# A new instruction order, a wider choice of engines, and a last output tile in two column halves, in clustered attention followed by a softplus feed-forward layer

## The chip, the cores and the metric

The kernel runs on one core of one Trainium2 chip. The metric is the device time of one execution in microseconds (us). The kernel before takes 824.29 us, the median of three runs (823.51 to 825.02). Engines are called PE (TensorE matmul), PEld (TensorE weight load), DVE (VectorE), ACT (ScalarE), POOL (GpSimd) and SP (SyncE, which here issues every DMA).

## The reference, cut to what matters

Attention with 4 batches, 8 heads, 768 positions and head size 64; a query sees only the keys that fall to the same one of 16 centroids. Its output, as 3072 tokens of 512, goes through a feed-forward layer of width 2048 with a softplus.

```python
mask = q_assign[:, :, :, None] == k_assign[:, :, None, :]
scores = scale * np.matmul(q, k.transpose(0, 1, 3, 2))
scores = np.where(mask, scores, -1000000000.0)
attn = np.exp(scores - np.max(scores, axis=-1, keepdims=True))
attn = attn / (np.sum(attn, axis=-1, keepdims=True) + 1e-09)
attn_out = np.matmul(attn, v)
x = attn_out.transpose(0, 2, 1, 3).reshape(B * S, H * D)
h = x @ w_in
g = np.maximum(h, 0.0) + np.log1p(np.exp(-np.abs(h)))
return g @ w_out
```

## The kernel before

Numbers of 32 bits are split into a high and a low half of 16 bits, so that a product takes three matmuls. Attention is done in 192 tiles of 128 queries by 768 keys (a "tile t" below), in 8 passes of 24 tiles; one pass is one batch and half of its positions. The heads of batch 0 are prepared at the start with transposes on PE (`turn` with `on_chip`), all later ones with DMA transposes (`flip`). The first 24 tiles are done in 32 bits with transposes on PE (`whole`, L992); the later ones transpose their probabilities by DMA (`pt<-phl`). The feed-forward layer of a pass runs beside the attention of the next one: `ffn1` (L1222) gives a piece h of 128 features, `softplus` (L1247) makes g of it on ACT, DVE and POOL, `ffn2` (L1304) multiplies by w_out, one half of the features at a time, and `store` (L1328) scales the result out of PSUM and sends it. The very last work is the tile i = 2 of the last pass, second half: 24 matmuls of 512 columns, one DVE instruction (L1339) and one DMA of 256 KB (L1342).

The order of all instructions is written out: every step of the work is a generator ("chain"), each `yield op(...)` is one step, and the list `SEQUENCE` names, one after another, the chain whose next step is emitted. A code is 1000 times the number of the engine chosen plus the number of the chain. So 465 is the next step of the first matrix (two steps for each of 128 pieces), 466 the next of the second, and 1465 cannot occur since such a step has one engine only. Chain 0 prepares the centroids, 1 to 48 are the loads and preparations of k, q and v, 49 to 432 are `scores(t)` and `attend(t)` in turn, 433 to 464 the weights (`prep_weights`, L626), and from 467 on stand chains that others spawn. Every engine takes its instructions in this order and waits by semaphores where its input is not there. The class `Order` (L269) follows the list with planned durations; its outcome matters for the code only through `warm` (L487), which puts small matmuls ("fill", L494) where PE is planned to idle.

Steps with a choice in the kernel before: `evict` (PSUM to SBUF copy, ACT or DVE, L514), `sub` (low half, POOL or DVE, L524), `cast` (high half, ACT, DVE or POOL, L534), the shift in `prep_weights` (L669, DVE or ACT), and three steps of `softplus` (L1263 to L1285). Steps with one engine only: the scaling in `prep_weights` (L663, ACT), the copy of k's high half (L822, ACT), the scaling of q (L918, ACT) and the product of q with its cluster flag (L977, POOL). In `prep_q` the step before L977 gives the flag `aq` (L968, DVE), and the step beside it writes the mask (L971, DVE); `prep_k` writes k's mask at L839 (DVE).

Of the kernel before, what the change touches and what calls it, by code (L numbers as in the profile page):

```python
# [19 lines left out]
SW2 = 256.0  # L20
# [8 lines left out]
WIDE = 1  # L29
EBIAS = 200  # L30
# [1384 lines left out]
```

## Time and profile before

| what | value |
|---|---|
| device time, median of 3 (lowest to highest) | 824.29 us (823.51 to 825.02) |
| profiled execution: span from first to last instruction | 824.5 us; what lies around it is not on the page |
| busy: PE, PEld, DVE, ACT, POOL | 98%, 63%, 79%, 69%, 54% |
| granted TensorE clock, mean | 0.998 |
| chain that ended last | PE 79%, DMA 4%, DVE 3%, ACT 3%, POOL 1%, issue 1% |

The page describes one profiled execution. "Busy" is the share of the span in which an engine has at least one instruction running; PE's matmuls overlap, so their durations add up to more than the busy time. A row of the waits says which engine sat idle, at which line, and which instruction ended the idle time.

### The profile page before, as it was taken

How to read it: one execution, taken by the hardware profiler on the slowest of the kernel's cores; microseconds unless marked ns; L12 is line 12 of the kernel's file. 1: busy time of each engine (PE TensorE's matmuls, PEld its weight loads, DVE VectorE, ACT ScalarE, POOL GpSimd, SP SyncE). 2: the span in 40 equal slices, each digit the busy share in tenths (PEclk: the TensorE clock that was granted, in tenths of full speed). 3: DMA queues.
4: the chain of work that ended last, by engine and by line, in shares of the span. 5: the costliest groups of instructions: out<-in, count | busy, mean ns of one | idle time of the engine just before them, and what ended most of it. 6: DMA issues, size and time to landing. Idle time of an engine off the chain costs nothing.

```text
span 824.5 us, 19467 instructions
## 1 busy us (share of the span) xinstructions
PE 809.5 (98%) x7893; PEld 518.3 (63%) x7893; DVE 647.6 (79%) x1127; ACT 567.8 (69%) x987; POOL 444.5 (54%) x358
## 2 busy tenths in 40 slices
PE   8999988999999999999999999999999999999998
PEld 7888865655656565656565656656666565555553
DVE  8999999998898977898778888887587887743222
ACT  7999998998857667667565746785686664433530
POOL 4325444655367376777685465856777653522320
PEclk9999999999999999999999999999999999999999
DMA  9436999999979999999978989999969874640001
GB/s 327 161 85 168 214 201 228 205 225 177 207 153 187 180 195 205 195 211 193 180 141 155 173 174 183 211 212 175 201 135 169 163 135 103 123 84 14 26 2 38
DMA packets 386314, 134.27 MB, mean 163 GB/s; under 512 B 362672, under 2 KB 379056, under 8 KB 386224
## 3 DMA queue, kind: packets, MB, share of 16 engines
q1 hardware_dynamic: 386224, 133.03, 80.1%
q8 instruction: 61, 1.00, 0.5%
q14 instruction: 29, 0.24, 0.1%
HBM read 35.68 MB, written 6.29 MB: 51 GB/s over the span
## 4 chain that ended last, share of the span: by engine, by line
PE 79%; DMA 4%; DVE 3%; ACT 3%; POOL 1%; issue 1%; DVEq 0%; ACTq 0%; POOLq 0%
PE s L1021 11%; PE h L1236 9%; PE h L1237 9%; PE h L1238 9%; PE o L1321 9%; PE o L1319 9%; PE o L1320 9%; DMA pt<-phl 4%; PE mbank L1157 3%; PE mbank L1159 3%; PE mbank L1158 3%; DVE negm L1037 1%; ACT p L1048 1%; DVE phl L529 1%; ACT phl L539 1%
## 5 line engine op out<-in xcount | busy, mean ns | idle before, releaser
L1048 ACT ACTIVATE p<-s,negm 128x768 f32<-128x768 f32 x190 | 171.9, 908 | 77.9 <-DVE negm L1037 65.6
L1037 DVE TENSOR_REDUCE negm<-s 128x1 f32<-128x768 f32 x192 | 181.7, 951 | 35.4 <-PE s L1021 34.2
L529 POOL TENSOR_TENSOR phl<-p,phl 128x768 f16<-128x768 f32 x81 | 138.2, 1710 | 71.7 <-DVE phl L539 36.0
L1238 PE MATMUL h<-xT,wi 128*128 128x384 f16 x512 | 166.8, 326 | 0.0
L1237 PE MATMUL h<-xT,wi 128*128 128x384 f16 x512 | 166.8, 326 | 0.0
L1236 PE MATMUL h<-xT,wi 128*128 128x384 f16 x512 | 166.7, 326 | 0.0
L1021 PE MATMUL s<-kt,qt 128*128 128x384 f16 x768 | 156.1, 326 | 2.5 <-DVE phl L1111 1.4
L1321 PE MATMUL o<-wo,gh 128*128 128x512 f16 x384 | 146.0, 380 | 0.0
L1320 PE MATMUL o<-wo,gh 128*128 128x512 f16 x384 | 146.0, 380 | 0.0
L1319 PE MATMUL o<-wo,gh 128*128 128x512 f16 x384 | 146.0, 380 | 0.0
L1285 POOL TENSOR_TENSOR fg<-fg,fa 128x384 f32<-128x384 f32 x64 | 69.8, 1094 | 82.9 <-ACT fa L1281 74.9
L1157 PE MATMUL mbank<-vb,pt 128*128 128x65 f16 x1008 | 109.0, 193 | 3.0 <-DMA pt<-phl 3.0
L1158 PE MATMUL mbank<-vb,pt 128*128 128x64 f16 x1008 | 109.1, 192 | 0.0
L1159 PE MATMUL mbank<-vb,pt 128*128 128x65 f16 x1008 | 108.8, 194 | 0.0
L1157 PEld LDWEIGHTS <-pt 128*128 128x128 f16 x1008 | 93.7, 98 | 16.8 <-DMA pt<-phl 5.1
L1021 PEld LDWEIGHTS <-qt 128*128 128x128 f16 x768 | 71.9, 98 | 48.9 <-issue 3.5
L1158 PEld LDWEIGHTS <-pt 128*128 128x128 f16 x1008 | 93.1, 97 | 11.4
L1267 ACT ACTIVATE fa<-h 128x384 f32<-128x384 f32 x82 | 40.2, 491 | 80.7 <-PE h L1238 63.8
L529 DVE TENSOR_TENSOR phl<-p,phl 128x768 f16<-128x768 f32 x81 | 90.6, 1125 | 4.3 <-ACT phl L539 2.2
L1159 PEld LDWEIGHTS <-pt 128*128 128x128 f16 x1008 | 93.2, 97 | 0.0
L539 ACT CAST phl<-p 128x768 f16<-128x768 f32 x92 | 75.2, 828 | 8.3 <-DMA pt<-phl 7.7
L1280 ACT ACTIVATE fa<-fa 128x384 f32<-128x384 f32 x128 | 65.8, 522 | 11.2 <-DVE fa L1263 11.1
(176 smaller groups left out, 1474.0 us busy)
## 6 DMA issues: line engine op xcount, KB each, us to landing
wo<-in_moe_w_in_dram SPq DMA_DIRECT2D x16, 512.0 KB, 6.8
wo<-in_moe_w_out_dram SPq DMA_DIRECT2D x14, 512.0 KB, 4.5
rawk<-in_k_dram SPq DMA_DIRECT2D x16, 384.0 KB, 4.2
rawq<-in_q_dram SPq DMA_DIRECT2D x16, 384.0 KB, 4.4
rawv<-in_v_dram SPq DMA_DIRECT2D x16, 384.0 KB, 4.6
out_dram<-ot SPq DMA_DIRECT2D x24, 256.0 KB, 2.6
pt<-phl SPq DMA_TRANSPOSE x82, 5.9
wraw<-in_moe_w_out_dram SPq DMA_DIRECT2D x2, 512.0 KB, 4.6
```

The source lines that it names most:

```text
L529: [lambda e=e: e.tensor_tensor(dst, a, b, ALU.subtract) for e in (nc.gpsimd, nc.vector)],
L1021: nc.tensor.matmul(st[:, j, :SH], qt[:, s, i], kt[:, s, NT // 2 * j : NT // 2 * (j + 1)], start=(s == 0), stop=(s == 1),)
L1037: yield op("DVE", 950, lambda: nc.vector.tensor_reduce(negm, st[:, :, :SH], AX.XY, ALU.max, negate=True))
L1157: nc.tensor.matmul(av, pt[:, 0, c], vb[:, c, D : 2 * D + 1], start=(c == 0), stop=False)
L1158: nc.tensor.matmul(av[:, :D], pt[:, 0, c], vb[:, c, :D], start=False, stop=False)
L1159: nc.tensor.matmul(av, pt[:, 1, c], vb[:, c, D : 2 * D + 1], start=False, stop=(c == NT - 1))
L1236: nc.tensor.matmul(hp, w[0], x[0], start=(c == 0), stop=False)
L1237: nc.tensor.matmul(hp, w[0], x[1], start=False, stop=False)
L1238: nc.tensor.matmul(hp, w[1], x[0], start=False, stop=(c == NP - 1))
L1319: nc.tensor.matmul(po, g[0], wo[:, f, 0, 0], start=(f == f0), stop=False)
L1320: nc.tensor.matmul(po, g[0], wo[:, f, 0, 1], start=False, stop=False)
L1321: nc.tensor.matmul(po, g[1], wo[:, f, 0, 0], start=False, stop=(f == f0 + NF // 2 - 1))
```

## The change

1. The planner's rule for steps that use the port of DVE and POOL (`shared=True`) is written anew: it keeps the last 64 users of either engine and lets the earlier request go first (`lock`). It is used while the program is written and adds no instruction.
2. Four steps get a choice of engine: L663 (ACT, DVE or POOL), L822 (the same), L918 (the same) and L977 (POOL or DVE); the shift L669 may also go to POOL, with another form of the next step.
3. The last tile of `ffn2` is done in two halves of 256 columns, each with its own eviction and its own DMA of 128 KB.
4. `SEQUENCE` is replaced as a whole. It has 3660 codes instead of 3654; the six more are four steps of `ffn2` and two of a second `store`.

The codes say which engine does each step. The main steps whose counts differ (those of L663 stay on ACT in all 32 cases, and none of the shifts goes to POOL):

| step | before | after |
|---|---|---|
| q scaling (L918) | ACT 18 | ACT 13, DVE 4, POOL 1 |
| copy of k's high half (L822) | ACT 12 | ACT 10, DVE 2 |
| q times flag (L977) | POOL 18 | POOL 11, DVE 7 |
| cast of p | ACT 92, DVE 26, POOL 44 | ACT 107, DVE 23, POOL 32 |
| cast of g | ACT 32, DVE 11, POOL 21 | ACT 25, DVE 22, POOL 17 |
| sub of g | DVE 34, POOL 30 | DVE 26, POOL 38 |
| cast of x, sub of x on DVE | 2, 8 | 8, 14 |
| cast of x, sub of x on POOL | 11, 24 | 5, 18 |
| cast of k on ACT, DVE, POOL | 14, 0, 2 | 11, 2, 3 |
| sub of k on DVE, POOL | 8, 8 | 11, 5 |
| sub of v on DVE, POOL | 7, 9 | 4, 12 |
| abs and relu of softplus on ACT, DVE | 167, 89 | 175, 81 |

Up to the step of DVE that ends tile 30 (L1111, its 234th step before, its 235th after) the two orders hold the same steps of DVE except: one eviction of a q transpose (384 wide) and the `sub` of weight step 0 go away, three evictions of k transposes (768 wide) come. ACT has up to the same tile three such evictions less, one of q more, one cast of k more and one cast of weights less. POOL has the `sub` of weight step 0 and a cast of weights more and a cast of k less. Around the flags of the first four heads DVE's order is:

```text
before: aq q0, L780 q2, L971 q0, L839 k2 ...    aq q2, L922 q4, L971 q2 ...
after:  aq q0, L839 k2, sub k6, L971 q0 ...     aq q2, L1037 t0, L678 w0, L874, L971 q2 ...
```

and the cast of k of heads 2 and 3, POOL's first large step before, is ACT's after. PE's order differs in most places by a few steps; the number of `ffn1` and `ffn2` steps ahead of `scores(t)` is the same at t = 24, 32, 40, 48, 60 and 96. SP's order up to tile 31 has the same transposes in the same order, apart from one of x that comes earlier; among the loads, that of v of heads 0 and 1 comes six places later, and a few neighbours are exchanged.

```diff
 SEQUENCE = [
-    0, 0, 0, 0, 0, 0, 0, 0, 0, 0, 1, 2, 4, 0, 1, 0, 6, 468, 469, 1001, 0, 468, 0, 0, 3, 1, 468, 2004, 1, 0, 468, 1,
...
+    466, 465, 1648, 647, 647, 466, 649, 1647, 465, 648, 466, 465, 466, 465, 466, 650, 650, 650, 650, 650, 465, 649,
...
+    1660, 1661, 2660, 660, 1663, 1663, 663, 663, 663, 1663, 466, 1663, 466, 664, 664, 466, 466, 466, 466, 665, 665,
+    466, 466, 466, 466, 666, 666, 466, 466, 466, 466, 667, 667,
 ]
...
-        self.shared = {"DVE": 0.0, "POOL": 0.0}
+        self.shared = {"DVE": [], "POOL": []}
...
+    def lock(self, eng, asked, ns):
+
+        other = self.shared["POOL" if eng == "DVE" else "DVE"]
+        start, later = asked, []
+        for i, x in enumerate(other):
+            if x[2] <= asked:
+                continue
+            if x[0] > asked:
+                later = other[i:]
+                break
+            start = max(start, x[2])
+        if later:
+            delay = start + ns - later[0][1]
+            if delay > 0:
+                self.free["POOL" if eng == "DVE" else "DVE"] += delay
+                for x in later:
+                    x[1] += delay
+                    x[2] += delay
+        self.shared[eng] = self.shared[eng][-63:] + [[asked, start, start + ns]]
+        return start
...
-        yield op("ACT", 660, lambda: nc.scalar.activation(mag, val, AF.Abs, scale=sc))
+        yield op(
+            ("ACT", "DVE", "POOL"),
+            (660, 420, PSC),
...
-            yield op("ACT", 830, lambda: nc.scalar.copy(n2[:, :, :D], n1[:, :, D:]))
+            yield op(
+                ("ACT", "DVE", "POOL"),
+                (830, DCP, PCP),
...
-        yield op("ACT", 120 + 720 * part, lambda: nc.scalar.activation(n1[:, :, :D], qf, AF.Copy, scale=SCALE))
+        yield op(
+            ("ACT", "DVE", "POOL"),
+            (120 + 720 * part, 145 + 420 * part, 178 + PQS * part),
...
-            "POOL",
-            180 + 1290 * part,
-            lambda: nc.gpsimd.tensor_tensor(n2[:, :, :D], n1[:, :, :D], aq.to_broadcast([P, nx, D]), ALU.mult),
+            ("POOL", "DVE"),
+            (180 + 1290 * part, 130 + DQA * part),
...
+        ends = pi == len(passes) - 1 and half and i == nt - 1
+        sides = [slice(0, DM // 2), slice(DM // 2, DM)] if ends else [slice(0, DM)]
+        for side in sides:
+            for fp in range(f0 // 2, f0 // 2 + NF // 4):
+                yield wait("g", pi, fp)
...
+                        out_ = po[:, side]
+                        nc.tensor.matmul(out_, g[0], wo[:, f, 0, 0, side], start=(f == f0), stop=False)
...
+            if ends and side is sides[0]:
+                od.spawn(store(pi, half, i, po, ok, side), od.cur["prio"])
+        od.spawn(store(pi, half, i, po, ok, sides[-1]), od.cur["prio"])
...
+            lambda: nc.vector.scalar_tensor_tensor(at, from_, 1.0 / SW2, at, ALU.mult, ALU.add),
+        )
+        if side.stop == DM:
+            od.drop(ok)
+        yield op("SP", 500, lambda: nc.sync.dma_start(out_v[b, :, c0 + i, side], at), load=share * 256e3 / 290)
```

## Rows read from the trace of the kernel before

**Rows 1.** First part of the page: busy time, share and instructions of each engine.
```profile
PE 809.5 (98%) x7893; PEld 518.3 (63%) x7893; DVE 647.6 (79%) x1127; ACT 567.8 (69%) x987; POOL 444.5 (54%) x358
```

**Rows 2.** Busy time by stretch: stretch, length, engines' busy us (instructions), clock, DMA share, GB/s.
```profile
5.60:20.00 14.40, 12.72 (x275) 11.96 (x274) 13.48 (x42) 13.42 (x22) 7.58 (x9) 1.00 1.04 382
20.00:113.00 93.00, 88.47 (x921) 76.32 (x920) 91.97 (x185) 91.69 (x180) 39.76 (x36) 1.00 0.64 165
130.00:821.00 691.00, 689.96 (x6477) 415.62 (x6475) 522.21 (x843) 443.44 (x754) 387.94 (x299) 1.00 0.82 157
821.50:824.50 3.00, 0.00 (x0) 0.00 (x0) 0.04 (x1) 0.00 (x0) 0.00 (x0) 1.00 0.23 87
```

**Rows 3.** The same view for PE's fill matmuls (L494) alone, 0 to 130 us.
```profile
sum 130.00, PE 16.92 PEld 14.57; mean PE 2.82 PEld 2.43
```

**Rows 4.** Waits of PE, whole run: total us, times, longest.
```profile
PE mbank L1157 <- DMA pt<-phl: 3.0, 3, 2.3
...
PE kT L744 <- DVE kn L839: 0.7, 1, 0.7
PE qT L744 <- DVE al L874: 0.6, 1, 0.6
```

**Rows 5.** Waits of PE from 130 us on.
```profile
PE mbank L1157 <- DMA pt<-phl: 0.8, 2, 0.4
```

**Rows 6.** Timeline, SP and PE, 98 to 134 us: start, us, instruction.
```profile
120.30 3.67 SPq L563 DMA_TRANSPOSE pt<-phl  x1
...
128.15 0.20 PE L1157 MATMUL mbank<-vb,pt 128*128 128x65 f16 x1 [2.25 <-DMA pt<-phl]
```

**Rows 7.** Timeline of the first 26 us, DVE and POOL.
```profile
8.22 0.85 DVE L598 TENSOR_TENSOR cb<-cn,cb 128x64 f16<-128x64 f32 x1
8.99 0.21 DVE L599 TENSOR_TENSOR cb<-cn,cb 128x64 f16<-128x64 f32 x1
...
18.91 0.82 POOL L977 TENSOR_TENSOR n<-qn,aq 128x384 f16<-128x384 f16 x1 [1.44 <-DVE aq L968]
...
18.95 0.84 DVE L839 TENSOR_SCALAR kn<-kn 128x192 f16<-128x192 f16 x1
...
23.75 0.20 DVE L839 TENSOR_SCALAR kn<-kn 128x192 f16<-128x192 f16 x1
...
24.76 0.81 DVE L971 TENSOR_SCALAR n<-n 128x96 f16<-128x96 f16 x1
```

**Rows 8.** Groups by line and shape: busy us, mean ns, idle before.
```profile
L520 ACT COPY kt<-kT 128x768 f16<-128x768 f16 x12 | 9.5, 804 | 0.9 <-PE kT L744 0.9
L520 DVE COPY kt<-kT 128x768 f16<-128x768 f16 x4 | 2.2, 551 | 0.0
L520 ACT COPY qt<-qT 128x384 f16<-128x384 f16 x10 | 5.1, 505 | 0.0
L520 DVE COPY qt<-qT 128x384 f16<-128x384 f16 x6 | 2.1, 349 | 0.0
L529 DVE TENSOR_TENSOR wi<-wo,wi 128x512 f16<-128x512 f32 x3 | 2.0, 682 | 0.0
L529 POOL TENSOR_TENSOR wi<-wo,wi 128x512 f16<-128x512 f32 x13 | 15.6, 1206 | 17.2 <-ACT wi L539 9.7 <-DVE wi L539 7.4
L1274 DVE TENSOR_SCALAR fg<-h 128x384 f32<-128x384 f32 x43 | 23.6, 549 | 9.2 <-ACT fa L1267 9.2
```

**Rows 9.** Timeline of the end, from 819 us on.
```profile
820.43 0.38 PE L1321 MATMUL o<-wo,gh 128*128 128x512 f16 x1
820.85 0.69 DVE L1339 SCALAR_TENSOR_TENSOR ot<-o,ot 128x512 f32<-128x512 f32 x1 [4.49 <-PE o L1321]
821.57 0.33 SPq L1342 DMA_DIRECT2D out_dram<-ot  x1
```

**Rows 10.** DMA issues by line: count, KB each, median us from issue to landing.
```profile
cf<-in_centroids_dram SPq DMA_DIRECT2D x1, 32.0 KB, 1.7
```

**Rows 11.** Busy time by stretch, columns as in Rows 2.
```profile
300.00:350.00 50.00, 50.00 (x527) 31.40 (x523) 38.55 (x69) 35.94 (x65) 36.10 (x29) 1.00 1.06 202
```

More of the change, by code (lines that the diff above doesn't have):

```diff
@@ L29 @@
 WIDE = 1
+PSC = 1560
+PQS = 1950
+DQA = 830
+DCP = 365
+PCP = 820
 EBIAS = 200
@@ L369, in pump, with start @@
         self.cur = outer
-    def start(self, ch, eng):
+    def lock(self, eng, asked, ns):
[17 more added lines that the diff above has]
+        return start
+    def start(self, ch, eng, ns):
         t = max(ch["now"], self.free[eng])
         if ch["op"][4].get("shared") and eng in self.shared:
-            t = max(t, self.shared["POOL" if eng == "DVE" else "DVE"])
+            t = self.lock(eng, t, ns)
         return t
@@ L383, in run @@
                 eng, ns, emit = eng[which], ns[which], emit[which]
-            start = self.start(ch, eng)
+            start = self.start(ch, eng, ns)
             if eng == "PE" and self.warm:
@@ L387, in run @@
             self.free[eng] = start + ns - self.PIPE[eng]
-            if opt.get("shared") and eng in self.shared:
-                self.shared[eng] = start + ns
             end = start + ns + self.LAT[eng]
@@ L662, in prep_weights, with zero @@
             yield wait("sc", gate)
-        yield op("ACT", 660, lambda: nc.scalar.activation(mag, val, AF.Abs, scale=sc))
+        yield op(
+            ("ACT", "DVE", "POOL"),
+            (660, 420, PSC),
+            (
+                lambda: nc.scalar.activation(mag, val, AF.Abs, scale=sc),
+                lambda: nc.vector.tensor_scalar(mag, val, sc, None, ALU.mult),
+                lambda: nc.gpsimd.tensor_scalar(mag, val, sc, None, ALU.mult),
+            ),
+            shared=True,
+        )
         od.set(("wd", step))
+        signs = []
+        def zero():
+            signs.append(1)
+            nc.gpsimd.tensor_scalar(val, val, 0.0, None, ALU.mult)
         yield op(
-            ("DVE", "ACT"),
-            (420, 770),
+            ("DVE", "ACT", "POOL"),
+            (420, 770, PSC),
             (
@@ L670, in prep_weights @@
                 lambda: nc.scalar.activation(low, top, AF.Relu, bias=down, scale=2.0**-13),
+                zero,
             ),
@@ L674, in prep_weights, with join @@
         )
-        yield op(
-            "DVE",
-            685,
-            lambda: nc.vector.scalar_tensor_tensor(high, high, -0x80000000, low, ALU.bitwise_and, ALU.bitwise_or),
-            shared=True,
-        )
+        def join():
+            if signs:
+                nc.vector.scalar_tensor_tensor(high, low, 29, high, ALU.logical_shift_right, ALU.bitwise_or)
+            else:
+                nc.vector.scalar_tensor_tensor(high, high, -0x80000000, low, ALU.bitwise_and, ALU.bitwise_or)
+        yield op("DVE", 685, join, shared=True)
         yield op(
@@ L821, in prep_k @@
             keys.append(k2)
-            yield op("ACT", 830, lambda: nc.scalar.copy(n2[:, :, :D], n1[:, :, D:]))
+            yield op(
+                ("ACT", "DVE", "POOL"),
+                (830, DCP, PCP),
+                (
+                    lambda: nc.scalar.copy(n2[:, :, :D], n1[:, :, D:]),
+                    lambda: nc.vector.tensor_copy(n2[:, :, :D], n1[:, :, D:]),
+                    lambda: nc.gpsimd.tensor_copy(n2[:, :, :D], n1[:, :, D:]),
+                ),
+                shared=True,
+            )
         h = n % H
@@ L917, in prep_q @@
         n1 = p2.tile([P, nx, P], F16, name=f"qn1_{sfx}", **own(k1, 2))
-        yield op("ACT", 120 + 720 * part, lambda: nc.scalar.activation(n1[:, :, :D], qf, AF.Copy, scale=SCALE))
+        yield op(
+            ("ACT", "DVE", "POOL"),
+            (120 + 720 * part, 145 + 420 * part, 178 + PQS * part),
+            (
+                lambda: nc.scalar.activation(n1[:, :, :D], qf, AF.Copy, scale=SCALE),
+                lambda: nc.vector.tensor_scalar(n1[:, :, :D], qf, SCALE, None, ALU.mult),
+                lambda: nc.gpsimd.tensor_scalar(n1[:, :, :D], qf, SCALE, None, ALU.mult),
+            ),
+            shared=True,
+        )
         yield op(
@@ L974, in prep_q @@
         yield op(
-            "POOL",
-            180 + 1290 * part,
-            lambda: nc.gpsimd.tensor_tensor(n2[:, :, :D], n1[:, :, :D], aq.to_broadcast([P, nx, D]), ALU.mult),
+            ("POOL", "DVE"),
+            (180 + 1290 * part, 130 + DQA * part),
+            [
+                lambda e=e: e.tensor_tensor(n2[:, :, :D], n1[:, :, :D], aq.to_broadcast([P, nx, D]), ALU.mult)
+                for e in (nc.gpsimd, nc.vector)
+            ],
             shared=True,
@@ L1308, in ffn2, with emit, store @@
         f0 = NF // 2 * half
-        for fp in range(f0 // 2, f0 // 2 + NF // 4):
-            yield wait("g", pi, fp)
-            for u in range(2):
-                yield wait("wr", NWI + 2 * fp + u)
-            gh = gt[pi, fp]
-            def emit(fp=fp, gh=gh):
-                for u in range(2):
-                    f = 2 * fp + u
-                    g = [gh[:, s, u, i * P : (i + 1) * P] for s in range(2)]
-                    nc.tensor.matmul(po, g[0], wo[:, f, 0, 0], start=(f == f0), stop=False)
-                    nc.tensor.matmul(po, g[0], wo[:, f, 0, 1], start=False, stop=False)
-                    nc.tensor.matmul(po, g[1], wo[:, f, 0, 0], start=False, stop=(f == f0 + NF // 2 - 1))
-            yield op("PE", 1300, emit)
-            if i == nt - 1:
-                od.set(gkey[pi, fp])
-        od.spawn(store(pi, half, i, po, ok), od.cur["prio"])
-    def store(pi, half, i, po, ok):
+        ends = pi == len(passes) - 1 and half and i == nt - 1
[3 more added lines that the diff above has]
+                yield wait("g", pi, fp)
+                for u in range(2):
+                    yield wait("wr", NWI + 2 * fp + u)
+                gh = gt[pi, fp]
+                def emit(fp=fp, gh=gh, side=side):
+                    for u in range(2):
+                        f = 2 * fp + u
+                        g = [gh[:, s, u, i * P : (i + 1) * P] for s in range(2)]
+                        out_ = po[:, side]
+                        nc.tensor.matmul(out_, g[0], wo[:, f, 0, 0, side], start=(f == f0), stop=False)
+                        nc.tensor.matmul(out_, g[0], wo[:, f, 0, 1, side], start=False, stop=False)
+                        nc.tensor.matmul(out_, g[1], wo[:, f, 0, 0, side], start=False, stop=(f == f0 + NF // 2 - 1))
+                yield op("PE", 1300 // len(sides), emit)
+                if i == nt - 1 and side is sides[-1]:
+                    od.set(gkey[pi, fp])
+            if ends and side is sides[0]:
+                od.spawn(store(pi, half, i, po, ok, side), od.cur["prio"])
+        od.spawn(store(pi, half, i, po, ok, sides[-1]), od.cur["prio"])
+    def store(pi, half, i, po, ok, side):
         b, c0, nt = passes[pi]
@@ L1337, in store @@
             return
+        share = (side.stop - side.start) / DM
+        at, from_ = acc[:, side], po[:, side]
         yield op(
-            "DVE", 680, lambda: nc.vector.scalar_tensor_tensor(acc, po, 1.0 / SW2, acc, ALU.mult, ALU.add)
-        )
-        od.drop(ok)
-        yield op("SP", 500, lambda: nc.sync.dma_start(out_v[b, :, c0 + i], acc), load=256e3 / 290)
-        od.set(ak)
+            "DVE",
+            130 + 550 * share,
+            lambda: nc.vector.scalar_tensor_tensor(at, from_, 1.0 / SW2, at, ALU.mult, ALU.add),
+        )
+        if side.stop == DM:
+            od.drop(ok)
+        yield op("SP", 500, lambda: nc.sync.dma_start(out_v[b, :, c0 + i, side], at), load=share * 256e3 / 290)
+        if side.stop == DM:
+            od.set(ak)
     def chain_of(gens):
```

323 rows, old and new, of the table SEQUENCE are left out of this document.

## The prediction

> **What bounds the kernel now.** I read the page's first part, then the busy time by stretch, then the waits of PE, and last the two ends of the timeline. PE is busy for 98% of the span [rows 1]. The stretches say where the rest is. From 130 us to 821 us PE is busy for 689.96 of 691.00 us, so this long part is set by PE's own work and nothing in it but about 1 us can be won [rows 2]; PE's waits there add up to 0.8 us [rows 5]. What PE loses, it loses before: 14.40 - 12.72 = 1.7 us between 5.6 and 20 us, 93.00 - 88.47 = 4.5 us between 20 and 113 us [rows 2], and part of what counts as busy is fill, 16.92 us of it up to 130 us [rows 3]. In the stretch from 20 to 113 us DVE is busy for 91.97 and ACT for 91.69 of 93.00 us [rows 2]: both are full at the same time, and POOL with 39.76 us is not. The start is therefore a stage in which VectorE and ScalarE bind, with PE close behind; what shortens it is less work on both of them, and less on one alone gives only what the other allows. PE's waits name DVE twice there, for the mask of k (0.7 us) and for a flag of a head (0.6 us) [rows 4]. The stage hands over to the PE-bound part at one wait of 2.25 us for the transposed probabilities, whose DMA SP issued at 120.30 us [rows 6]; it moves with whatever is ahead of it. At the other end, after the last matmul, stand one DVE instruction of 0.69 us and one DMA, issued at 821.57 us, with which the span ends at 824.5 us [rows 9].
>
> **The change, part by part.** The sum is made against the profiled span of 824.5 us; the median of the runs is 824.29 us, 0.2 us less, and I carry that difference over.
>
> *The planner's port rule and the new choices as such* add no instruction and cost nothing. L663 stays on ACT in all 32 cases and no shift goes to POOL, so that part of the wider choice isn't used at all.
>
> *The start, by counts.* I compare the steps in both orders up to the DVE step that ends tile 30. DVE loses one eviction of q (0.349) and one `sub` of weights (0.682) and gains three evictions of k (0.551 each): 1.653 - 1.031 = +0.62 us [rows 8]. ACT loses three such evictions (0.804 each) and gains one of q (0.505): -1.91 us; one cast comes and one goes, which I set at nothing, since both are one pass over a tile of the same kind [rows 8]. POOL gains that `sub` (1.206) [rows 8]; it is busy for 39.76 of 93 us [rows 2], and that free time is the cover; without it the 1.2 us would be DVE's or ACT's.
>
> *The start, by waits inside DVE steps.* Three DVE steps of the first 26 us last far longer than their like, each beside a POOL step: L598 takes 0.85 where its sister L599 takes 0.21; L839 takes 0.84 from 18.95 us, while a POOL step runs from 18.91 for 0.82, and 0.20 at 23.75 us; L971 takes 0.81 at 24.76 us [rows 7]. A DVE step of this kind that starts after POOL's waits until POOL's ends. That is 0.64 + 0.64 + 0.61 = 1.9 us, taking 0.20 as the free duration of L971 as well, which is narrower than L839. In the new order the cast of k on POOL, which stood beside L598, is ACT's: I take the 0.64 as gone. L971 of heads 2 and 3 comes four steps after its flag instead of two, behind a reduction of a whole tile and two more steps: I take it that POOL's product, 0.82 us long for the heads before, has ended by then, 0.61 gone. L839 of heads 2 and 3 still comes right behind the flag that starts POOL's product, and so does a `sub`: nothing gone. Together -1.25 us, bounds 0 (none goes, other pairs meet instead) and -1.9 (all go). New pairs that the order makes can't be read from rows of before; the upper bound covers as many as go.
>
> So DVE: +0.62 - 1.25 = -0.6 us, from +0.6 to -1.3; ACT: -1.9 us. The one that is relieved less sets the stage: **-0.6 us**. Whether it reaches the end: the transposes that follow stand in the same order on SP, and the DMA of the hand-over waits for the same steps, so the 2.25 us of PE's wait [rows 6] go along with it. SP's loads are exchanged by a few places; v of heads 0 and 1 is loaded six places later, behind w and other v; it is read first by the first product with v, behind transposes and scores of the first tile. I cost it at nothing; if it came too late PE would wait for it as at the hand-over, 2.25 us at the most [rows 6], and that is inside rival D.
>
> *The long middle.* PE has the same matmuls in a slightly different order: nothing to win but the 0.8 us of [rows 5], and I take 0. DVE gains 7 products of q, some casts and subs of x and casts of g, and loses subs of g; with the durations of their like that is about 12 us over a stage in which it is busy for 522.21 of 691.00 us [rows 2]: 77% instead of 76%. The cover is DVE's free time of about 169 us. It isn't even: in the stretch that holds the work of 300 to 350 us the new order puts about 7 us more on DVE (six sums and five relus more, at 0.55 to 0.65 each, and single steps that about cancel against casts and abs that leave), and 38.55 of 50.00 us [rows 11] become about 46.
>
> *The tail.* The last tile's 24 matmuls of 512 columns become 48 of 256, with the same number of columns. The 24 more weight loads cost 518.3 / 7893 = 0.066 us each [rows 1] if nothing hid them, 1.6 us; from 130 to 821 us, 415.62 us of loads lie beside a PE that is busy throughout [rows 2], so I take 0. The first half is evicted and sent while the second is computed. What stays behind the last matmul is an eviction of 256 columns and 128 KB. Eviction: 512 columns take 0.69 [rows 9], 384 columns 0.549 [rows 8], so 0.14 for 128 columns, and 256 take about 0.41: -0.28 us. DMA: it took 824.5 - 821.57 = 2.9 us from issue to the end [rows 9]; in the 3.00 us around it the DMA engines were busy for 0.23 of the time, 0.69 us [rows 2], the rest is latency that doesn't scale with size; half of 0.69 is -0.34 us. Bounds: 0 if nothing scales; and by the nearest smaller transfer, 32 KB in 1.7 us [rows 10], (2.9 - 1.7) x 128 / 224 = -0.69. I take -0.34, since it is measured on the same transfer. Tail: **-0.6 us**, from -0.3 to -1.0.
>
> Sum: 824.5 - 0.6 - 0.6 = 823.3 us of span, and by the median 824.29 - 1.2 = **823.0 us**.
>
> **The rivals.**
> *A, the forecast:* 823.0 us, with its own range from 824.29 - 2.3 = 822.0 (DVE gains 1.3, tail 1.0) to 824.29 - 0.3 = 824.0 (DVE 0, tail 0.3); for its waits in DVE steps speak three rows, against it that they lie within the first 26 us only.
> *B, only the tail pays:* the port waits come back in other pairs, DVE's 0.62 us stay, and 824.29 + 0.6 - 0.6 = 824.3 us. For it: L839 and the `sub` still stand behind the flag.
> *C, the stage follows ACT:* DVE avoids all three waits and more beyond, ACT's 1.9 us come through, PE's small waits of the middle (0.8) go too and the tail gives 1.0: 824.29 - 3.7 = 820.6 us. For it: ACT and DVE are full together [rows 2], and the new plan counts the port's waits, which the old one counted by emission order. Against it: DVE has more work by count.
> *D, DVE becomes late in the middle, slower than before:* in stretches where it is loaded to 46 of 50 us a row maximum or a low half comes late, PE's next scores wait, and such a wait costs what the one at the hand-over costs, 2.25 us [rows 6]. One gives 824.29 - 1.2 + 2.2 = 825.3, two 827.5 us; it decides from the point at which DVE's free 4 us of a stretch are used up, that is with two or three blocked steps of the 0.64 us kind [rows 7] beside one late input. The Trainium skill, page "SBUF — State Buffer", section "Who interferes with whom", says that the pair of ports which DVE and GpSimd share is an exclusive lock for a whole instruction, that the later one blocks fully, and that ScalarE never waits for anyone. By that rule the eight steps that leave ACT for DVE (four scalings of q, two copies and two casts of k), and the seven products that leave POOL, are liable to a block that they were not liable to before or that was POOL's; the rows of L839 and L971 agree with it. Eight blocks of 0.64 us would be 5 us on DVE, which its free time hides unless they fall together.
>
> **How the numbers follow.** Chances: A 0.48, B 0.14, C 0.22, D 0.16. The predicted time is A's, 823.0 us. The range reaches down past C and up past D's single wait: 820.3 to 825.8 us, which leaves out what lies beyond in C and D's second wait, about 0.2. About 0.2% (1.65 us) is what a measurement of this kernel can tell from no change: faster is below 822.64 us, slower above 825.94 us. Below 822.64 lie C and two fifths of A: 0.22 + 0.20 = 0.42. Above 825.94 lies most of D, 0.13. The rest, 0.45, is within 0.2%.
>
> **What would show it.** In the profile after: the last DVE instruction at about 0.4 us and the span's end some 0.6 us closer to the last matmul (the tail); L598 and L971 near 0.2 us, L839 once near 0.84 (the port); the end of PE's wait for `pt` at 128.15 us, and the DMA issued at 120.30 us, some 0.6 us earlier (the start); PE's busy time from 130 us on still within 1 to 2 us of the stretch (the middle). The prediction is wrong if the start shifts by more than 1.5 us either way, if PE waits in the middle for DVE, or if the wait at the hand-over grows past the 2.25 us.

## The result, and the profile after

| | before | after |
|---|---|---|
| median of five runs, us | 824.57 (823.51 to 826.22) | 834.02 (832.95 to 836.12) |
| ratio, 95% interval | 1 | 1.0114 (1.01 to 1.0128) |
| profiled span, us | 824.5 | 832.2 |
| first product with transposed p that waits for its DMA [rows 6] | 128.15 | 127.16 |
| last matmul starts [rows 9] | 820.43 | 828.87 |
| from there to the end of the span | 4.1 | 3.3 |

The changed kernel is 1.1% slower, 9.4 us, where 823.0 was forecast. The last three lines of the table say where: the start is 1.0 us shorter (128.15 to 127.16) and the tail 0.7 us, and between the two points the same matmuls take 828.87 - 127.16 = 701.71 us in place of 820.43 - 128.15 = 692.28. **The middle lost 9.4 us**, the part on which the forecast had set nothing.

The page's first part (it answers [rows 1]) and the stretches of [rows 2], with 300 to 350 us [rows 11] and one more stretch of the middle; columns as there:

```profile
PE 811.7 (98%) x7915; PEld 519.8 (62%) x7915; DVE 635.6 (76%) x1149; ACT 573.7 (69%) x988; POOL 409.1 (49%) x336
```

```profile
5.60:20.00 14.40, 13.00 (x278) 11.83 (x277) 13.08 (x43) 12.76 (x21) 5.61 (x5) 1.00 1.04 382
20.00:113.00 93.00, 89.13 (x917) 76.31 (x914) 91.20 (x184) 90.85 (x178) 41.11 (x39) 1.00 0.65 164
...
130.00:821.00 691.00, 682.54 (x6439) 411.52 (x6438) 509.85 (x861) 450.73 (x756) 351.25 (x275) 1.00 0.82 157
300.00:350.00 50.00, 50.00 (x512) 31.09 (x511) 43.86 (x82) 34.51 (x59) 24.23 (x20) 1.00 1.03 199
410.00:460.00 50.00, 48.71 (x506) 30.34 (x505) 37.26 (x60) 31.38 (x52) 26.36 (x20) 1.00 0.83 151
```

The first part hardly shows the change: PE is at 98% in both. The stretches do: from 130 to 821 us PE is busy for 682.54 of 691.00 us where it was busy for 689.96. And they already speak against the rival that the prediction had for this side. DVE is busy for 43.86 us of the 50 from 300 on, near the 46 that were foreseen, and there PE loses nothing. It loses 1.3 us from 410 to 460 us, where DVE has 12.7 us free. Over the whole middle DVE is busy for 12.4 us less than before, not for 12 us more.

Waits of PE from 130 us on (total us, times, longest), which were 0.8 us before [rows 5]:

```profile
PE s L1083 <- ACT p L1110: 2.3, 5, 0.9
PE mbank L1219 <- DMA pt<-phl: 2.0, 2, 1.1
PE o L1385 <- ACT fg L1337: 1.5, 2, 1.0
PE mbank L1219 <- DVE x L1254: 0.9, 1, 0.9
PE h L1298 <- ACT fg L1337: 0.8, 2, 0.5
PE o L1385 <- DVE ot L1411: 0.5, 1, 0.5
PE sim_q L802 <- DVE al L924: 0.4, 1, 0.4
PE h L1298 <- DVE fg L1336: 0.3, 1, 0.3
```

Together they are 8.7 us. No single wait is long; there are 15 of them, on ACT (4.6 us), on DVE (2.1 us) and on a DMA (2.0 us). What most of them have in common, as the runs below show, is one step back. Each pair of tiles writes its split probabilities into a buffer `phl`, of which there are two, and SP transposes it by DMA into `pt`. The `cast` that begins the next pair but one has to wait until that transpose has landed. Here is what all casts waited for (idle time of their engine just before them, by what ended it: us, times), first before (L539), then after (L562):

```profile
  DMA pt<-phl: 25.2, 19
```

```profile
  DMA pt<-phl: 49.9, 28
```

Twice as much, and on other engines: ACT's casts of p waited 7.7 us from 140 us on before and 27.6 after, DVE's 0.9 and 6.3, POOL's 16.5 and 15.3. POOL, busy for 49% of the span, has the most time to spare; on ACT, which frees PE's banks, everything that stands behind the cast in ACT's order waits too. The timeline shows one case (start, us, instruction, and in brackets the idle time before it and what ended it):

```profile
455.07 8.59 SPq L586 DMA_TRANSPOSE pt<-phl  x2
```

```profile
458.00 0.51 ACT L1343 ACTIVATE fa<-fa 128x384 f32<-128x384 f32 x1
462.25 0.83 ACT L562 CAST phl<-p 128x768 f16<-128x768 f32 x1 [3.73 <-DMA pt<-phl]
462.99 0.89 ACT L1110 ACTIVATE p<-s,negm 128x768 f32<-128x768 f32 x1
463.78 0.48 ACT L1329 ACTIVATE fa<-h 128x384 f32<-128x384 f32 x1
464.15 0.52 ACT L1342 ACTIVATE fa<-fa 128x384 f32<-128x384 f32 x1
464.57 0.49 ACT L1337 ACTIVATE fg<-h 128x384 f32<-128x384 f32 x1
```

```profile
462.22 0.20 PE L1219 MATMUL mbank<-vb,pt 128*128 128x65 f16 x1 [0.85 <-DMA pt<-phl]
465.10 0.38 PE L1385 MATMUL o<-wo,gh 128*128 128x512 f16 x1 [0.48 <-ACT fg L1337]
```

SP issues the transpose at 455.07 us. It lands at 462.2, and at that moment two things go on: PE's product, which had waited 0.85 us for the same transpose, and ACT's cast, before which ACT had stood idle for 3.73 us. The relu (L1337) four steps behind the cast is the last to read the PSUM bank that PE needs next, and PE waits 0.48 us more.

### The profile page after: what moved, and what is told of

Its sections match the earlier page's. It is cut to its first block, busy times and chain, and to the rows that moved or that the text cites. A ratio compares the mean times of both kernels' runs of the same rounds, so it can differ in the third digit from the quotient of the medians.

```text
span 832.2 us, 19551 instructions
## 1 busy us (share of the span) xinstructions
PE 811.7 (98%) x7915; PEld 519.8 (62%) x7915; DVE 635.6 (76%) x1149; ACT 573.7 (69%) x988; POOL 409.1 (49%) x336
## 4 chain that ended last, share of the span: by engine, by line
PE 71%; DMA 9%; DVE 8%; ACT 7%; issue 3%; POOL 1%; SPq 0%; DVEq 0%; ACTq 0%; POOLq 0%
PE s L1083 10%; PE o L1385 9%; PE o L1387 9%; PE o L1386 8%; PE h L1298 8%; DMA pt<-phl 8%; PE h L1300 8%; PE h L1299 8%; PE mbank L1219 3%; PE mbank L1221 3%; PE mbank L1220 3%; ACT p L1110 2%; DVE negm L1099 2%; PE mbank L1215 1%; ACT phl L562 1%
## 5 line engine op out<-in xcount | busy, mean ns | idle before, releaser
L552 POOL TENSOR_TENSOR phl<-p,phl 128x768 f16<-128x768 f32 x81 | 134.2, 1664 | 78.1 <-ACT phl L562 46.5
L1385 PE MATMUL o<-wo,gh 128*128 128x512 f16 (+1 forms) x392 | 146.8, 374 | 2.0 <-ACT fg L1337 1.5
L1387 PE MATMUL o<-wo,gh 128*128 128x512 f16 (+1 forms) x392 | 146.9, 375 | 0.0
L1386 PE MATMUL o<-wo,gh 128*128 128x512 f16 (+1 forms) x392 | 146.8, 375 | 0.0
L1347 POOL TENSOR_TENSOR fg<-fg,fa 128x384 f32<-128x384 f32 x64 | 66.8, 1047 | 117.5 <-ACT fa L1343 107.3
L562 ACT CAST phl<-p 128x768 f16<-128x768 f32 x107 | 88.3, 834 | 30.8 <-DMA pt<-phl 28.3
L552 DVE TENSOR_TENSOR phl<-p,phl 128x768 f16<-128x768 f32 x81 | 83.8, 1042 | 7.2 <-POOL phl L562 3.6
L1329 ACT ACTIVATE fa<-h 128x384 f32<-128x384 f32 x87 | 42.3, 488 | 64.8 <-PE h L1300 47.7
L552 POOL TENSOR_TENSOR gh<-fg,gh 128x768 f16<-128x768 f32 x38 | 63.1, 1662 | 38.1 <-DVE gh L562 20.5
```

The lines of the kernel that those rows point to most:

```text
L552: [lambda e=e: e.tensor_tensor(dst, a, b, ALU.subtract) for e in (nc.gpsimd, nc.vector)],
L1385: nc.tensor.matmul(out_, g[0], wo[:, f, 0, 0, side], start=(f == f0), stop=False)
L1386: nc.tensor.matmul(out_, g[0], wo[:, f, 0, 1, side], start=False, stop=False)
L1387: nc.tensor.matmul(out_, g[1], wo[:, f, 0, 0, side], start=False, stop=(f == f0 + NF // 2 - 1))
```

## The experiments

Theories. **A**: the casts of p that wait for a `phl` buffer at the head of ACT's and DVE's queues. **B**: DVE late by its own load, its port or the new choices (the prediction's rival D). **C**: the new order as a whole leaves PE's inputs no margin, the buffer being one place of several. Ratios are to the kernel before, measured beside each.

### The tail alone

Four more steps of `ffn2` and a second store at the end of the order of before, and these two functions as in the change:

```diff
+        ends = pi == len(passes) - 1 and half and i == nt - 1
+        sides = [slice(0, DM // 2), slice(DM // 2, DM)] if ends else [slice(0, DM)]
...
+    466, 466, 466, 466, 667, 667,
```

> The kernel before with one edit: the last output tile is computed, added up and sent in two column halves. Engine choices and the order of everything else are those of before. Every theory on the slowdown lies in the middle, so all expect the tail's own gain: 0.6 us, from 0.3 to 1.0, that is about 824.0 us beside 824.6. More than 826 would say that the halves themselves cost something (24 more weight loads).

Measured: 825.49 us, ratio 0.9996 (0.9984 to 1.0007), 0.3 us faster with an interval that takes in 0. The profile is clearer: from the start of the last matmul to the end of the span 823.9 - 820.56 = 3.3 us, against 4.1. The halves do what was forecast, and no cost of theirs shows.

### Order without choices, choices without order

A code that keeps its place in the order and changes its engine, here the cast of tile 50, which goes back from ACT to POOL (454 such codes in the first run, the same 454 the other way round in the second, the 82 of the casts of p in the third):

```diff
-    149,
+    2149,
```

> The changed kernel with its order and its halves, but each step that both kernels have runs on the engine that it had before (454 steps differ). If the new choices of engine are the cause (casts of p that wait for their buffer on ScalarE and VectorE instead of GpSimd, or products and scalings of q on VectorE), the 9.5 us go and the time is 823 to 826 us. If the new order by itself is the cause, whatever the engines, it stays at 832 to 836 us. The order was searched together with its choices, so a third outcome is open: well over 836 us, where order and choices only make sense together.

> The reverse: the order of before, with the halves, and each step on the engine that the changed kernel gives it. If the choices alone cost the 9.5 us, 832 to 836 us; if the order alone does, 823 to 826 us; if they only make sense together, over 836 us.

> The changed kernel with one kind of step put back: the 82 casts of p that run on another engine than before (34 left GpSimd for ScalarE or VectorE, 22 came to it) run where they ran before. Theory A (the casts of p wait for one of the two phl buffers at the head of ScalarE's and VectorE's queues and hold up what stands behind them): the waits of ScalarE for that buffer fall from 28 us to about 8, and at least 6 of the 9.5 us come back, 824 to 828 us. Theory B (VectorE has too much since products and scalings of q are there): unchanged, 832 to 836 us. Theory C (the new order is too tight wherever the casts run): unchanged or slower, 832 us and more.

Measured: 952.25 us, ratio 1.1538 (1.15 to 1.1577), for the new order with the old choices; 879.66, 1.0652 (1.0629 to 1.0675), for the old order with the new choices; 861.41, 1.0434 (1.0408 to 1.046), for the changed kernel with the old engines of its 82 casts of p. All are far slower than either kernel, the third outcome that the first two expectations had left open. By the letter 861.41 us is also what C expected of the third run, but it lies 27 us above the changed kernel, so the mixture adds losses of its own. The three therefore decide nothing between A, B and C, and they don't say whether the order or the choices cost the 9.4 us: here each fits only the other. The casts of p in particular can't be put back by themselves.

### Cutting the two kernels in time

The list starts with the codes of one kernel that its plan puts before 140 us and goes on with all that are left, in the order of the other. In the first and third run it begins as the changed kernel's and ends, but for the halves, as that of before:

```diff
-    0, 0, 0, 0, 0, 0, 0, 0, 0, 0, 1, 2, 4, 0, 1, 0, 6, 468, 469, 1001, 0, 468, 0, 0, 3, 1, 468, 2004, 1, 0, 468, 1,
+    0, 0, 0, 0, 0, 0, 1, 0, 0, 0, 1, 0, 2, 468, 0, 0, 469, 4, 1001, 1, 468, 1, 468, 468, 0, 0, 1, 4, 469, 469, 469,
...
```

> Order and engine choices of the changed kernel for the first 140 us, those of before for the rest, and the halves of the last tile. PE loses 2.5 us less than before in the changed kernel's first 140 us, by the starts of its instructions, and the tail gives about 0.5. If the whole loss lies in the middle's order and choices, this one gets both gains and none of the loss: 824.6 - 2.5 - 0.5 = 821.6 us (821 to 822.5). If the changed start leaves something that is paid later (other wait states, transfers that come later), 824 us or more.

> The reverse: order and choices of before for the first 140 us, those of the changed kernel from there to the end. If the loss lies in the middle's order and choices: 834.0 + 2.5 = 836.5 us (835 to 838). If it comes from what the changed start does to the middle: about 824 us.

> The hybrid of e5 once more with more rounds: the changed kernel's order and choices for the first 140 us, those of before behind, and the halves of the last tile. If start and tail both pay, 0.3% (2.5 us) faster than before; if only the tail pays, 0.05% (0.4 us); the interval of e5 reached from 0.25% faster to the same.

Measured: the changed start with the old middle 824.15 us, ratio 0.9988 (0.9975 to 1.0001), and in the second series 824.22, 0.9984 (0.997 to 0.9999); the old start with the new middle 835.64, 1.0122 (1.0097 to 1.0146). Order and choices go together in such a cut, and it works: the loss belongs to the middle, whichever start stands before it. By the letter 824.15 us is the other outcome of the first expectation, a start that is paid for later. The profiles speak against that: from the hand-over's product to the last matmul the two runs with the changed start take 691.86 and 692.76 us, the kernel before 692.28, and the run with the new middle 702.18. The waits of PE from 130 us on in the first of them, beside the eight lines above:

```profile
PE o L1382 <- DVE ot L1408: 0.5, 1, 0.5
PE mbank L1216 <- DMA pt<-phl: 0.3, 1, 0.3
```

In this kernel start and tail together give 0.12 to 0.16%, 1.0 to 1.3 us, not the 3.0 that its expectation had. The 2.5 us for the start in it were read from the profiled execution of before, which had lost 1.7 us to a lower clock behind its hand-over (last section). It is the fastest of the versions that leave nothing out, though its lead on the kernel before is no more than the intervals can just tell.

### A third phl buffer

```diff
-            key = yield from ring("phl", 2)
+            key = yield from ring("phl", 3)
...
-        gkey[pi, fp] = yield from ring("g", NF // 2)
+        gkey[pi, fp] = yield from ring("g", 7)
...
-            accs[pi, i] = p2.tile([P, DM], F32, name=f"ot_{b}_{c0 + i}", **own(ak, QT)), ak
+            accs[pi, i] = ot2[:, min(i, 1)], ak
```

In both runs of this pair the last two of each three output tiles share one accumulator, so they don't hold their own sums; the work is the same. The DMA scratch (`DDS`) is cut from 1024 to 256 as well. Some pieces of w_out and of k (batch 0) use the same buffers as `phl`, so the third buffer loosens these too.

> The changed kernel, order and choices untouched, with three buffers for the split probabilities (phl) instead of two; the room comes from one of eight g buffers, from two output accumulators in place of three, and from the DMA scratch. Theory A (steps that wait at the head of ScalarE's, VectorE's and GpSimd's queues for a phl buffer, which only the landing of a transpose frees): their waits for it fall from 50 us to under 10 and PE gets most of its 11 us back, 824 to 828 us. Theory B (VectorE is late by its own load) and theory C (the order leaves PE's inputs no margin against any lateness, this buffer being one of several): under B unchanged, 832 us and more; under C a part, 828 to 832 us.

> The changed kernel with the room made for the third phl buffer (seven g buffers, output tiles two and three in one accumulator so that these two don't hold their own sums, less DMA scratch), but with two phl buffers as before. If that room costs nothing, 833 to 835 us, and the 5.5 us that the third buffer gave are its own. If it costs something, over 835 us, and the third buffer gave more than that.

Measured: 829.81 us, ratio 1.0047 (1.0033 to 1.0061), with the third buffer, and 836.44, 1.0134 (1.0114 to 1.0153), with the same room made and two buffers. So the buffer itself is worth 836.44 - 829.81 = 6.6 us by the medians, which are of two series, and 0.0087 of the time, 7.2 us, by the ratios; what the room cost, some 2 us by the ratios (1.0134 against 1.0114), lies within the intervals. The wait of casts for `DMA pt<-phl` is gone from the list (49.9 us after, 47.2 in the control). That is theory A at work, and for some two thirds of what the control loses. It isn't all: 829.81 us lies in the range that C had (828 to 832), not in A's, and of PE's waits from 140 to 821 us 5.5 us are left, among them

```profile
PE mbank L1218 <- DMA pt<-phl: 1.7, 3, 0.6
PE h L1297 <- DVE al L923: 1.2, 1, 1.2
```

The first line is products that wait for the transpose itself, which a third `phl` buffer doesn't touch. The second is DVE's port. With the buffer free, POOL's step comes earlier and meets two steps of DVE (three lines of DVE, then POOL, then the same two steps of DVE in the changed kernel):

```profile
189.30 1.28 DVE L717 SCALAR_TENSOR_TENSOR wraw<-wraw 128x512 int32<-128x512 int32 x1
190.50 2.01 DVE L550 TENSOR_TENSOR xn<-x,xn 128x384 f16<-128x384 f32 x1
...
194.90 0.19 DVE L923 TENSOR_SCALAR al<-sim_k 128x32 f16<-128x32 f32 x1
```

```profile
189.18 0.82 POOL L560 CAST phl<-p 128x768 f16<-128x768 f32 x1
190.09 2.00 POOL L550 TENSOR_TENSOR phl<-p,phl 128x768 f16<-128x768 f32 x1
```

```profile
190.08 0.68 DVE L719 SCALAR_TENSOR_TENSOR wraw<-wraw 128x512 int32<-128x512 int32 x1
190.67 0.55 DVE L552 TENSOR_TENSOR xn<-x,xn 128x384 f16<-128x384 f32 x1
```

The same two steps take 1.28 and 2.01 us beside POOL and 0.68 and 0.55 without, 2.1 us more together, and PE waits 1.2 us for the flag that DVE makes a few steps later. So B's mechanism exists, and in a kernel without margin one such meeting reaches PE; in the changed kernel itself the longest wait for such a flag is 0.4 us. Over the whole run the same 81 subtractions on DVE even take less time than before (busy us, mean ns; first before, then after):

```profile
L529 DVE TENSOR_TENSOR phl<-p,phl 128x768 f16<-128x768 f32 x81 | 90.6, 1125 | 4.3 <-ACT phl L539 2.2
```

```profile
L552 DVE TENSOR_TENSOR phl<-p,phl 128x768 f16<-128x768 f32 x81 | 83.8, 1042 | 7.2 <-POOL phl L562 3.6
```

### Transposes that land sooner

```diff
-            pt.rearrange("p u s c t -> p (u s c) t"), phl.rearrange("p u s j t -> p (u s j t)"), 4 * NT
+            pt.rearrange("p u s c t -> p (u s c) t")[:, NT:], phl.rearrange("p u s j t -> p (u s j t)")[:, S:], 4 * NT
-            pts[t - 1 + w] = pt[:, w], ptk
+            pts[t - 1 + w] = pt[:, 1], ptk
```

> The changed kernel, order, choices and buffers untouched; each DMA transpose of p moves 18 of its 24 blocks (the high half of the even tile is left out, and the even tile's product with v reads the odd tile's probabilities, so that PE does the same matmuls). What it tells apart: with three quarters of the blocks each transpose should land 1 to 1.5 us sooner (it takes 6.0 us now). Theory C (the new order leaves the steps behind these transposes no margin: casts that wait for the phl buffer and products that wait for pt): most of PE's 11 us of the middle come back, 824 to 827 us. Theory B (VectorE and its port, or the other choices, are late by themselves): less than 2 us come back, 832 us and more.

> The same edit on the kernel before. Its middle has next to nothing to win (PE's waits add up to 0.8 us), so theory C expects 0 to 1.5 us, 823 to 825 us; if it gains as much as the changed kernel does from the edit, the gain says nothing of the change.

Measured: the changed kernel 823.18 us, ratio 0.997 (0.996 to 0.9981); the kernel before 822.09, ratio 0.9962 (0.9949 to 0.9975). The medians from issue to landing (last column), after and then with 18 blocks:

```profile
pt<-phl SPq DMA_TRANSPOSE x82, 6.1
```

```profile
pt<-phl SPq DMA_TRANSPOSE x82, 4.8
```

With 1.3 us less per transpose, and the order, the choices, the buffers and PE's matmuls as they were, the changed kernel wins 0.0144 of the time, 11.9 us, and the kernel before 3.1 us. What the two differ by falls from 1.14% to 0.08%, 0.7 us, and each of these ratios has an interval of some 0.1% to either side. Some of either gain is the start's: the hand-over waits for such a transpose too, and in the changed kernel its product runs at 124.68 us instead of 127.16, 2.5 us of the 11.9. Here are the product and the last matmul, first of the changed kernel, then of the kernel before, both with 18 blocks:

```profile
124.68 0.20 PE L1217 MATMUL mbank<-vb,pt 128*128 128x65 f16 x1 [0.32 <-DMA pt<-phl]
...
817.75 0.27 PE L1385 MATMUL o<-wo,gh 128*128 128x256 f16 x1
```

```profile
125.71 0.19 PE L1153 MATMUL mbank<-vb,pt 128*128 128x65 f16 x1
...
816.08 0.38 PE L1317 MATMUL o<-wo,gh 128*128 128x512 f16 x1
```

From the one to the other the changed kernel takes 817.75 - 124.68 = 693.1 us instead of 701.7, 8.6 us less, and the kernel before 816.08 - 125.71 = 690.4 instead of 692.3, 1.9 us less. So the edit takes 6.7 of the 9.4 us of the middle away, and **2.7 us stay**; the times of the runs differ by less because the changed kernel's shorter start and tail hide part of it. The kernel before gains twice the 1.5 us that were expected, since its hand-over wait of 2.25 us [rows 6], which the expectation had left out, goes as well. Theory B can't explain what went away: nothing was taken from DVE. It isn't excluded for what stayed: of the 1.8 us of waits that PE still has from 130 us on in the changed kernel, 1.6 are for DVE. The edit also lowers the DMA traffic, from 157 to 134 GB/s between 130 and 821 us; but no wait of PE there was for any other DMA. The casts' waits for the landing fall from 49.9 to

```profile
  DMA pt<-phl: 20.4, 15
```

**So most of the middle's loss, 6.7 of 9.4 us, is the time by which transposes of p land too late for the new order**, the larger part by way of the `phl` buffer (A), another by the products that wait for `pt` (C). What makes the last 2.7 us isn't shown.

How little margin there is can be counted in the two traces. For 79 casts that begin a pair, the time from the landing that frees their buffer to their own start: within 0.3 us, which is taken to mean that the cast stood waiting, for 20 before and 36 after; the median is 1.7 and 0.8 us. The transpose itself is hardly slower, 5.9 us before and 6.1 after from issue to landing in the median, but it spreads from 5.4 to 8.2 us before and from 5.4 to 8.7 after. Why it spreads the runs don't show. The old order has room for that spread in most places.

The new order is tight by its own plan. The class `Order`, followed with its planned durations, puts such a cast within 0.3 us of the planned landing for 13 of 78 pairs before and for 34 after, and it ends at 824.1 us before and 822.8 us after. So by the plan the change is a gain of 1.4 us. The plan gives every transpose of 24 blocks the same duration, though the measured ones spread, and the changed kernel took 834.02 us. That this is why the plan failed is argued here, not run.

## Why the prediction was wrong, point by point

**The step that failed** is, of the long middle, "PE has the same matmuls in a slightly different order: nothing to win but the 0.8 us of [rows 5], and I take 0". The runs showed 9.4 us lost there, most of them by transposes of p that land too late for casts and products at the head of their engines' orders. The prediction costed the middle by sums: how many steps each engine gains or loses, and how much free time it has. For DVE the sum was wrong in its sign but on the safe side: 77% of the stretch was put instead of 76%, and it is 509.85 of 691.00 us, 74%, since many of DVE's steps became shorter, as the 81 subtractions above; 46 of 50 us were foreseen in the busiest stretch and 43.86 came. But free time in a sum isn't margin at a place. The loss arises where a step waits at the head of its engine for a landing, with the engine idle and ready work behind it; in such a place an engine's free time is the damage and not the cover.

**What was in sight.** The table of the change had 15 more casts of p on ACT and 12 fewer on POOL, and the trace of before had the waits of casts for `DMA pt<-phl`, 25.2 us of them. The prediction read the waits of PE alone in this part, which were 0.8 us, and never asked what ACT or DVE wait for and with how much room. A count of casts against transposes in the new list, or of their planned distances, would not have given 9.4 us, but it would have given a rival with another place.

**Rival D** had the sign, with a chance of 0.16, and the wrong mechanism: not one or two waits of 2.25 us of a DVE whose free time is used up, but 15 waits of 0.3 to 1.1 us, through ACT and the DMA more than through DVE, where DVE had time. It priced one or two places; there were many. Its place, the stretch from 300 to 350 us, is free of loss. Of the Trainium skill's rule that it drew on (page "SBUF — State Buffer", section "Who interferes with whom", an exclusive lock between DVE and GpSimd), the run with the third buffer shows a case, 2.01 us for a step of 0.55; most of the loss isn't made by it, and of the 2.7 us that stay it isn't shown.

**The tail** was right in its steps. After the last matmul (L1387) stand these two instructions, which answer [rows 9]:

```profile
829.18 0.42 DVE L1411 SCALAR_TENSOR_TENSOR ot<-o,ot 128x256 f32<-128x256 f32 x1 [2.87 <-PE o L1387]
829.63 0.33 SPq L1415 DMA_DIRECT2D out_dram<-ot  x1
```

The eviction of 256 columns takes 0.42 us (0.41 foreseen), and from the issue of the DMA to the end of the span it is 832.2 - 829.63 = 2.6 us, 0.3 less than before (0.34 foreseen).

**The start** came out near its -0.6, by mixed evidence. The waits inside DVE's steps went as foreseen for L598 (now L621) and for L971 of heads 2 and 3 (now L1030); the block beside POOL's product moved from L839 (now L889) to L1030 of the first heads, which answers [rows 7]:

```profile
9.13 0.23 DVE L621 TENSOR_TENSOR cb<-cn,cb 128x64 f16<-128x64 f32 x1
...
17.96 0.20 DVE L889 TENSOR_SCALAR kn<-kn 128x192 f16<-128x192 f16 x1
18.94 0.81 DVE L1030 TENSOR_SCALAR n<-n 128x96 f16<-128x96 f16 x1
...
25.10 0.18 DVE L1030 TENSOR_SCALAR n<-n 128x96 f16<-128x96 f16 x1
```

The transpose of the hand-over is issued at 119.69 us instead of 120.30 [rows 6], 0.6 us earlier, and PE's wait there is 1.12 us instead of 2.25:

```profile
119.69 4.20 SPq L586 DMA_TRANSPOSE pt<-phl  x1
...
127.16 0.20 PE L1219 MATMUL mbank<-vb,pt 128*128 128x65 f16 x1 [1.12 <-DMA pt<-phl]
```

But these are single executions, and the old start varies by as much: in the kernels with the old start and the full transposes that wait ends at 128.15, 127.13 and 127.28 us, in the two cuts with the new one at 126.43 and 126.20, in the changed kernel at 127.16, and in the runs with the third buffer and its control at 126.50 and 127.53. Their means differ by 0.8 us, their ranges overlap. The times of the two cuts, 1.0 and 1.3 us below the kernel before, agree with the 1.2 us that the forecast had for start and tail together, and can't be split between them.

So two of the three terms of the sum held, as far as single executions tell, and the one that was set at nothing decided.

## What to carry to other kernels

When all engines follow one written order, cost a new order by its margins and not by its sums: list for every step that waits on a DMA or on one of two buffers how long before its start the release comes, and ask what stands behind it on its engine. A wait that is harmless on an engine with nothing behind it can be dear on the one that also frees PE's banks, as in the case at 462 us; no run isolates this part. To find out which part of such an order pays, cut it in time: swapping choices in a fixed order measured here only that the two belong together. And where the order comes from a plan with fixed durations, compare their spread in a trace with the distances that the plan leaves.

## What the hardware showed that was not expected

- A DMA transpose of 24 blocks takes from 5.4 to 8.7 us to land (median 6.1 by the page). With 18 blocks the median is 4.8: about 0.2 us a block, an estimate worked out as (6.1 - 4.8) / 6, and 0.9 us beside it.
- In the profile of before, PE counts as fully busy in a stretch in which its clock is halved, right behind the wait of 2.25 us at 128.15 us. The first line is before, the second the same stretch of the kernel with the old start and the new tail (columns as in [rows 2], the clock is the number behind POOL's):

```profile
129.50:133.00 3.50, 3.50 (x13) 1.79 (x12) 3.37 (x5) 3.26 (x6) 1.27 (x1) 0.51 0.80 159
```

```profile
129.50:133.00 3.50, 3.50 (x21) 1.78 (x19) 3.37 (x6) 3.50 (x6) 1.65 (x1) 1.00 1.10 207
```

  13 matmuls in place of 21, at 0.51 of the clock, which is the lower of its two levels, 1.2 GHz. The cut with the old start doesn't show it either, behind a wait of 1.93 us. About half of the 3.5 us, 1.7 us, of the profiled execution of before is lost there under the name of busy time. It doesn't change the size of the middle's loss: three other profiled executions of the old middle, none with this fall of the clock, take 693.43 (the tail alone), 691.86 and 692.76 us (the two cuts) from the hand-over to the last matmul, against 692.28, and the new middle takes 701.71 and 702.18.
